# The second feed-forward matmul of seven token tiles as Strassen's seven block products

## The chip, the cores and the metric

One core of a Trainium2 chip. The metric is device microseconds of one execution; a kernel is run several times, beside runs of the kernel before on the same chip. Nearly all runs were fast. Fast runs of one kernel on one chip differ by up to about 1.5% (305.61 to 309.91 us for the kernel before).

In the views, PE is TensorE's matmuls, PEld its weight loads, DVE is VectorE, ACT ScalarE, POOL GpSimd and SP SyncE. A timeline line has start, length (both us), engine, source line, operation, output<-input, shapes and count; in brackets stands how long the engine was idle before it, and what ended that. "..." marks lines left out.

## The reference

Eight batches of eight heads do decayed linear attention ("retention") over 576 positions of width 64. The result, 4608 tokens of width 512, goes through a feed-forward block:

```python
ret = (q @ k.T / sqrt(64)) * gamma ** (i - j)   # i >= j, else 0
x = (ret @ v)                                    # 4608 x 512
h = x @ w_in                                     # 512 -> 2048
g = h * cos(h)
out = g @ w_out                                  # 2048 -> 512
```

## The kernel before

The tokens are handled in ten tiles n = 0 to 9, of 512 tokens (tiles 1 and 2: 256). Each tile has a first matmul, 8 blocks that fill a PSUM buffer of 128x1024 fp32 each (the text calls these buffers banks, by their names a, b, m, n and st), with a cosine on ScalarE and a multiply on VectorE behind every block, and a second matmul. The retention work of tile n + 1 is put between the matmuls of the second one: score matmuls, their mask products on VectorE, state matmuls, and "units" that do the output of two groups of 128 tokens.

```python
def mm1(n, et, c0, w, bank, inside={}):          # one block of the first matmul
    ...
    for j in range(m):
        for dg in range(DG):
            nc.tensor.matmul(ps[:, j, :], lhsT=w_in_sb[:, dg, ...], rhs=xT[:, dg, c0 : c0 + w], ...)
    cosh = cosp.tile([P, m, w], F32, tag="cosh", name="cosh")
    nc.scalar.activation(cosh, ps, ACTF.Sin, bias=half_pi, scale=1.0)
    nc.vector.tensor_mul(gT[:, et : et + m, c0 : c0 + w], ps, cosh)

def mm2(n, tsi, et, c0=0, c1=DM):                # one of 16 x 4 of the second matmul
    ...
    nc.tensor.matmul(ps, lhsT=gT[:, et, tsi * P : (tsi + 1) * P], rhs=w_out_sb[:, et, c0:c1], ...)
    if et == ET - 1:
        nc.scalar.copy(ot, ps)
        nc.sync.dma_start(out[...], ot)
        feed(s)                                  # more loads, preparations, transposes

def unit(g, bank, more=True, soon=False):
    attn_out([g, g + 1], bank, nc.scalar.copy)
    copy = states([g + 1, g + 2])()              # state matmuls into bank "st", additions on VectorE
    if more:
        scores2(g + 2)                           # scores into banks "a" and "b", then mask products
    copy()                                       # casts of the state, VectorE
# ... cut
```

GpSimd scales and casts q, k and v as they land (`prep`: two products of 1.04 us and a cast of 0.61 us for each group of 128 tokens). The program gives each engine its instructions in a fixed order, so an instruction that has to wait holds up those behind it in the same queue.

Of the kernel before, what the change touches and what calls it, by code (L numbers as in the profile page):

```python
# [8 lines left out]
F32 = mybir.dt.float32  # L9
# [4 lines left out]
ALU = mybir.AluOpType  # L14
# [3 lines left out]
def kernel(  # L18
# [38 lines left out]

    consts = ctx.enter_context(tc.tile_pool(name="consts", bufs=1))
    first = ctx.enter_context(tc.tile_pool(name="first", bufs=1))
    ld = ctx.enter_context(tc.tile_pool(name="ld", bufs=6))  # L60
    nat = ctx.enter_context(tc.tile_pool(name="nat", bufs=8))
    trp = ctx.enter_context(tc.tile_pool(name="trp", bufs=8))
    retp = ctx.enter_context(tc.tile_pool(name="retp", bufs=4))
    stp = ctx.enter_context(tc.tile_pool(name="stp", bufs=2))
    gp = ctx.enter_context(tc.tile_pool(name="gp", bufs=2))
    cosp = ctx.enter_context(tc.tile_pool(name="cosp", bufs=3))
    op = ctx.enter_context(tc.tile_pool(name="op", bufs=4))
    xp = ctx.enter_context(tc.tile_pool(name="xp", bufs=3))

    psum = ctx.enter_context(tc.tile_pool(name="psum", bufs=1, space=bass.MemoryType.PSUM))  # L70

# [150 lines left out]
        )  # L222
        tiles["sb", g + 1] = sb

    def states(gs):



        gs = [g for g in gs if g < NG and g % PER != PER - 1]
        if not gs:  # L230
            return lambda: (lambda: None)
        ps = psum.tile([P, len(gs), HG, D], F32, tag="st", name="st")
        for x, g in enumerate(gs):
            qks, vb, qkT, qT = tiles["a", g]
            vs = v_odd[:, g // PER % 2] if g % PER == MIX else vb
            for hg in range(HG):
                for he in range(2):
                    nc.tensor.matmul(  # L238
                        ps[he * D : he * D + D, x, hg, :],
                        lhsT=qks[:, 1, 2 * hg + he, :],  # L240
                        rhs=vs[:, 2 * hg + he, :],
                        start=(x == 0 and hg == 0),
                        stop=(x + 1 == len(gs) and hg == HG - 1),
                        skip_group_check=True,
                    )

        def copy():
            for g in gs:
                s, sb = tiles.pop(("s32", g)), blocks4[g % 4]
                for he in range(2):  # L250
                    r = slice(he * D, he * D + D)
                    nc.vector.tensor_copy(sb[r, :, r], s[r])  # L252
                tiles["sb", g + 1] = sb

        def add():
            for x, g in enumerate(gs):
                s = stp.tile([P, HG, D], F32, tag="s32", name="s32")
                if g % PER in (0, MIX):
                    nc.vector.tensor_copy(s, ps[:, x])  # L259
                else:  # L260
                    nc.vector.tensor_tensor(out=s, in0=ps[:, x], in1=tiles["s32"], op=ALU.add)  # L261
                tiles["s32"] = tiles["s32", g] = s
            return copy

        return add
# [61 lines left out]
        nc.scalar.activation(cosh, ps, ACTF.Sin, bias=half_pi, scale=1.0)  # L327
        nc.vector.tensor_mul(gT[:, et : et + m, c0 : c0 + w], ps, cosh)  # L328

    def mm2(n, tsi, et, c0=0, c1=DM):  # L330
        gT = tiles["g", n]
        if et == 0:
            bank = {0: "nmnm", 1: "nm", 2: "mn"}.get(n, "mnan")[tsi] if c0 == 0 else "ba"[c0 % DM // P % 2]
            tiles["o", tsi] = psum.tile([P, c1 - c0], F32, tag=bank, name="o")
        ps = tiles["o", tsi]
        nc.tensor.matmul(  # L336
            ps,
            lhsT=gT[:, et, tsi * P : (tsi + 1) * P],
            rhs=w_out_sb[:, et, c0:c1],
            start=(et == 0),  # L340
            stop=(et == ET - 1),
        )
        if et == ET - 1:
            ot = op.tile([P, c1 - c0], F32, tag="o", name="ot")
            nc.scalar.copy(ot, ps)  # L345
            s = starts[n] // P + tsi
            nc.sync.dma_start(out[s * P : (s + 1) * P, c0:c1], ot)
            feed(s)

    loaded = prepared = transposed = 4  # L350

# [144 lines left out]
    def unit(g, bank, more=True, soon=False):  # L496

        attn_out([g, g + 1], bank, nc.scalar.copy)
        copy = states([g + 1, g + 2])()
        if soon:  # L500
            copy()
        if more:
            scores2(g + 2)
        if not soon:
            copy()

    late = []
    for n, w in enumerate(widths):

        if n in (0, 3):  # L510
            halves = [(h, et) for et in range(0, ET, 4) for h in range(2)]
            if n == 3:
                halves.sort()
            blocks = [(et, half * 256, 256) for half, et in halves]
        elif n == 1:
            blocks = [(et, half * P, P) for half in range(2) for et in (0, 8)]
        else:
            blocks = [(et, 0, w) for et in range(0, ET, 1024 // w)]
        banks = {0: "abmabmab", 1: "bmba", 2: "bmab", 3: "mamabmab"}.get(n, "abmabmab")
        for i, (et, c0, cw) in enumerate(blocks):  # L520

            inside = {
                (0, 0): {2: lambda: (attn_out([3], "n"), state(3))},
                (1, 0): {4: lambda: scores(5, "a")},
                (1, 1): {3: lambda: attn_out([5], "a", evac=nc.scalar.copy)},
            }.get((n, i), {})
            mm1(n, et, c0, cw, banks[i], inside)
            if (n, i) == (3, 1):
                late.pop()()

        g = starts[n] // P + w // P
        if n == 0:
# [8 lines left out]
        elif n == 1:  # L541
            todo = pair(6, "ab", 16, 27)
        elif n == 2:
            todo = [(11, lambda: scores2(g)), (25, lambda: unit(g, "m", soon=True))]
            late += [lambda: unit(g + 2, "b", False)]
        elif n + 1 < len(widths):
            todo = [
                (20, lambda: unit(g, "m")),
                (52, lambda: unit(g + 2, "m", n > 3)),
            ]  # L550
            if n in (3, 4):
                todo[0] = (25, lambda: unit(g, "m"))
                todo.append((12, lambda: scores2(g)))
        else:
            todo = []
        todo.sort(key=lambda u: u[0])
        order, cols = [], [(0, DM)]
        for tsi in range(w // P):
            if (n + 1, tsi + 1) == (len(widths), w // P):
                cols = [(0, DM // 2), (DM // 2, 3 * DM // 4), (3 * DM // 4, DM)]  # L560
            order += [(tsi, et, c0, c1) for c0, c1 in cols for et in range(ET)]
        if n == 0:

            part = 3 * ET // 4
            order[: 2 * ET] = [
                (tsi, et, 0, DM)
                for tsi, et in [(t, e) for e in range(part) for t in range(2)]
                + [(t, e) for t in range(2) for e in range(part, ET)]
            ]
        for i, (tsi, et, c0, c1) in enumerate(order):  # L570
            while todo and todo[0][0] <= i:
                todo.pop(0)[1]()
            mm2(n, tsi, et, c0, c1)
        assert not todo


# [28 lines left out]
```

## Time and profile before

| | before |
|---|---|
| median of the first three runs | 309.84 us |
| median with the fourth, taken beside the changed kernel | 308.94 us |
| span of the profiled execution | 304.4 us |
| TensorE, VectorE, GpSimd busy | 97%, 57%, 33% |
| a late tile (6), first matmul to first matmul | 31.13 us |

From the page of the kernel before: busy time by engine, the granted TensorE clock in 40 slices (9 is full speed) and the chain of work that ended last, by engine.

```profile
span 304.4 us, 5826 instructions
...
PE 295.5 (97%) x2411; PEld 169.2 (56%) x2441; DVE 172.9 (57%) x215; ACT 128.2 (42%) x145; POOL 101.1 (33%) x127
...
PEclk9999999999999999999999999999999999999999
...
PE 92%; DMA 5%; issue 1%; SPq 1%; DVE 0%; POOL 0%; ACT 0%; ACTq 0%
```

TensorE is the bound: it is busy for 97% of the span; it is 92% of the chain.

One group of instructions, the multiplies of the first matmul (busy us, mean ns of one, idle before them):

```profile
L328 DVE TENSOR_TENSOR gT<-h,cosh 128x1024 bf16<-128x1024 f32 x72 | 88.2, 1225 | 54.4 <-ACT cosh L327 54.3
```

A group's mean for TensorE is a modelled duration (379 ns for 512 columns), not a pitch: for matmuls the spacing is read from the timeline, 215.9 ns for 512 columns and 109.2 ns for 256. The multiply of VectorE, 1.225 us, comes every 1.73 us in the first matmul, so 0.5 us of every block is free.

A line of the view of one source line, the casts of the state on VectorE, gives the shortest, the median and the longest duration; below it the timeline where GpSimd is busy, and then where it is not.

```profile
L252 DVE CAST sb<-s x48: 274/291/1182, 82.6 to 266.3; 64x256 bf16<-64x256 f32 x48
```

```profile
148.53 1.04 POOL L136 TENSOR_TENSOR qks<-fq,gq 128x512 bf16<-128x512 f32 x1 [2.23 <-DMA fq<-in_q_dram]
...
148.84 3.07 DVE L252 CAST sb<-s 64x256 bf16<-64x256 f32 x4
...
149.72 1.04 POOL L137 TENSOR_TENSOR qks<-fk,gk 128x512 bf16<-128x512 f32 x1
```

```profile
171.49 1.20 DVE L252 CAST sb<-s 64x256 bf16<-64x256 f32 x4
```

Four casts beside GpSimd's work took 3.07 us, four casts without it 1.20 us.

The table of stretches, one line for each of tiles 2, 3 and 4 (us, busy time and count of each engine, granted clock, DMA share, GB/s):

```profile
core 0: us, PE busy (x) PEld busy (x) DVE busy (x) ACT busy (x) POOL busy (x), PEclk, DMA share, GB/s
67.50:83.94 16.44, 16.22 (x163) 11.19 (x165) 9.28 (x13) 6.54 (x7) 8.08 (x9) 1.00 1.21 206
83.94:117.04 33.10, 32.73 (x342) 23.22 (x344) 23.90 (x32) 14.20 (x15) 16.73 (x19) 1.00 1.08 213
117.04:148.83 31.79, 31.26 (x242) 15.91 (x245) 18.56 (x20) 13.27 (x14) 14.34 (x17) 1.00 1.21 221
```

### The profile page before, as it was taken

The numbers are of one execution on the slowest core, as the hardware profiler recorded it, in microseconds if no ns is written. First come the engines' busy times: TensorE is split into PE (matmuls) and PEld (weight loads), VectorE is DVE, ScalarE is ACT, GpSimd is POOL, SyncE is SP. The second block draws the span as 40 slices with busy tenths as digits, with TensorE's granted clock in tenths as the row PEclk, the third lists the DMA queues.
The fourth block names the chain that finished last, engine by engine and source line by source line (L and its number), as shares of the span: only waits on it lengthen the run. The fifth ranks groups of instructions, "written<-read, shape, count | busy, mean of one in ns | idle before, by whom it ended". The sixth has DMA issues, their size and how long they took to land.

```text
span 304.4 us, 5826 instructions
## 1 busy us (share of the span) xinstructions
PE 295.5 (97%) x2411; PEld 169.2 (56%) x2441; DVE 172.9 (57%) x215; ACT 128.2 (42%) x145; POOL 101.1 (33%) x127
## 2 busy tenths in 40 slices
PE   8899999999999999999999999999999999999995
PEld 3578647758588554445544554455445544554444
DVE  5677514665687665774875566646765557504700
ACT  2656333515256224532364236422652255226511
POOL 2780076445346355444536253415330000000000
PEclk9999999999999999999999999999999999999999
DMA  8999999999989999999999999389923600020012
GB/s 208 202 209 207 208 219 194 220 228 203 209 181 207 220 216 248 228 221 195 223 242 223 187 263 196 49 196 210 254 35 86 89 34 2 34 71 34 0 71 69
DMA packets 150810, 50.19 MB, mean 165 GB/s; under 512 B 140800, under 2 KB 146304, under 8 KB 150784
## 3 DMA queue, kind: packets, MB, share of 16 engines
q1 hardware_dynamic: 146560, 45.63, 79.6%
q0 software_dynamic: 4224, 4.19, 8.4%
q8 instruction: 19, 0.31, 0.5%
q14 instruction: 7, 0.06, 0.1%
HBM read 36.70 MB, written 9.44 MB: 152 GB/s over the span
## 4 chain that ended last, share of the span: by engine, by line
PE 92%; DMA 5%; issue 1%; SPq 1%; DVE 0%; POOL 0%; ACT 0%; ACTq 0%
PE h L319 41%; PE o L336 40%; PE ov L292 3%; PE sc L179 3%; DMA w_in_sb<-in_moe_w_in_dram 2%; DMA fk<-in_k_dram 2%; PE ov L279 2%; PE st L238 1%; SPq L111 1%; PE st L208 0%; DVE xT L304 0%; POOL qks L137 0%; SPq L381 0%; PE tr L157 0%; ACT ot L345 0%
## 5 line engine op out<-in xcount | busy, mean ns | idle before, releaser
L336 PE MATMUL o<-w_out_sb,gT 128*128 128x512 bf16 (+2 forms) x586 | 126.2, 367 | 2.5 <-issue 2.2
L319 PE MATMUL h<-xT,w_in_sb 128*128 128x512 bf16 (+2 forms) x826 | 127.1, 313 | 0.7 <-DMA w_in_sb<-in_moe_w_in_dram 0.2
L328 DVE TENSOR_TENSOR gT<-h,cosh 128x1024 bf16<-128x1024 f32 x72 | 88.2, 1225 | 54.4 <-ACT cosh L327 54.3
L319 PEld LDWEIGHTS <-w_in_sb 128*128 128x128 bf16 x832 | 75.9, 98 | 50.4 <-issue 0.4
L327 ACT ACTIVATE cosh<-h,half_pi 128x1024 f32<-128x1024 f32 x72 | 80.2, 1113 | 51.3 <-PE h L319 51.3
L336 PEld LDWEIGHTS <-gT 128*128 128x128 bf16 x608 | 56.3, 98 | 62.0 <-issue 0.2
L136 POOL TENSOR_TENSOR qks<-fq,gq 128x512 bf16<-128x512 f32 x32 | 33.3, 1042 | 98.0 <-DMA fq<-in_q_dram 95.4
L345 ACT COPY ot<-o 128x512 f32<-128x512 f32 (+2 forms) x38 | 21.4, 563 | 86.4 <-PE o L336 86.3
L137 POOL TENSOR_TENSOR qks<-fk,gk 128x512 bf16<-128x512 f32 x35 | 36.5, 1043 | 16.2 <-DMA fk<-in_k_dram 14.4
L188 DVE TENSOR_TENSOR ret<-sc,tri 128x1024 bf16<-128x1024 f32 x32 | 38.0, 1218 | 4.1 <-PE sc L179 4.0
L304 ACT CAST xT<-ov 128x1024 bf16<-128x1024 f32 (+1 forms) x18 | 16.5, 917 | 21.4 <-PE ov L292 21.2
L143 POOL CAST vb<-fv 128x512 bf16<-128x512 f32 x32 | 19.6, 612 | 6.9 <-DMA fv<-in_v_dram 5.5
L261 DVE TENSOR_TENSOR s<-st,s 128x256 f32<-128x256 f32 x18 | 7.6, 424 | 24.3 <-PE st L238 24.0
L252 DVE CAST sb<-s 64x256 bf16<-64x256 f32 x48 | 19.2, 401 | 0.7
L292 PE MATMUL ov<-ret,vb 128*64 128x128 bf16 x288 | 12.0, 222 | 0.0
L217 DVE TENSOR_TENSOR sb<-st,diag 128x512 bf16<-128x512 f32 x8 | 5.5, 686 | 11.4 <-PE st L208 10.6
L259 DVE COPY s<-st 128x256 f32<-128x256 f32 x6 | 2.5, 424 | 15.8 <-PE st L238 15.8
L179 PEld LDWEIGHTS <-qkT 64*128 64x128 bf16 x288 | 8.1, 94 | 5.0 <-ACT qkT L162 2.3
L279 PEld LDWEIGHTS <-sb 128*128 128x128 bf16 x128 | 8.4, 98 | 3.8
L179 PE MATMUL sc<-qkT 64*128 64x128 bf16 x256 | 10.3, 217 | 0.0
L292 PEld LDWEIGHTS <-vb 128*64 128x64 bf16 x288 | 8.7, 109 | 2.0
L279 PE MATMUL ov<-qkT,sb 128*128 128x128 bf16 (+1 forms) x116 | 8.8, 215 | 0.1
(53 smaller groups left out, 76.3 us busy)
## 6 DMA issues: line engine op xcount, KB each, us to landing
out_dram<-ot SPq DMA_DIRECT2D x35, 256.0 KB, 4.2
fk<-in_k_dram SPq DMA_DIRECT2D x32, 256.0 KB, 4.8
fv<-in_v_dram SPq DMA_DIRECT2D x32, 256.0 KB, 5.0
fq<-in_q_dram SPq DMA_DIRECT2D x28, 256.0 KB, 4.1
w_in_sb<-in_moe_w_in_dram POOLq DMA_DIRECT2D x4, 512.0 KB, 8.6
w_out_sb<-in_moe_w_out_dram POOLq DMA_DIRECT2D x4, 512.0 KB, 15.9
fq<-in_q_dram SPq DMA_DIRECT2D x2, 512.0 KB, 4.4
fq<-in_q_dram SPq DMA_DIRECT2D x8, 128.0 KB, 4.2
```

The lines of the kernel that those rows point to most:

```text
L136: nc.gpsimd.tensor_tensor(out=qks[:, 0], in0=fq, in1=tq, op=ALU.mult)
L137: (nc.vector if g == 3 else nc.gpsimd).tensor_tensor(out=qks[:, 1], in0=fk, in1=tk, op=ALU.mult)
L143: nc.gpsimd.tensor_copy(vb, fv)
L179: nc.tensor.matmul(ps[:, he, hg, :], lhsT=qkT[d0 : d0 + D, HG + hg, :], rhs=qT[d0 : d0 + D, hg, :], start=True, stop=True,)
L188: nc.vector.tensor_tensor(out=ret.rearrange("p a b i -> p (a b) i"), in0=ps.rearrange("p a b i -> p (a b) i"), in1=mask.unsqueeze(1).to_br ...
L279: nc.tensor.matmul(ps[:, x, hg, :n], lhsT=sb[:, hg, :], rhs=qT[:, hg, :n], start=(hg == 0), stop=False, skip_group_check=True,)
L292: nc.tensor.matmul(ps[he * D : he * D + D, x, hg, :], lhsT=vb[:, 2 * hg + he, :], rhs=ret[:, he, hg, :], start=(g % PER == 0 and hg == 0), ...
L319: nc.tensor.matmul(ps[:, j, :], lhsT=w_in_sb[:, dg, (et + j) * P : (et + j + 1) * P], rhs=xT[:, dg, c0 : c0 + w], start=(dg == 0), stop=(d ...
L327: nc.scalar.activation(cosh, ps, ACTF.Sin, bias=half_pi, scale=1.0)
L328: nc.vector.tensor_mul(gT[:, et : et + m, c0 : c0 + w], ps, cosh)
L336: nc.tensor.matmul(ps, lhsT=gT[:, et, tsi * P : (tsi + 1) * P], rhs=w_out_sb[:, et, c0:c1], start=(et == 0), stop=(et == ET - 1),)
L345: nc.scalar.copy(ot, ps)
```

## The change

For the tiles from 3 on (`S7 = 3`), the second matmul `C = G W` is done in seven products of half-size blocks in place of eight. Blocks are sums of bf16 operands; products that share a sum stay in one fp32 PSUM chain. Products run in the order 3, 4, 5, 2, 1, 7, 6. Each needs a sum of two quarters of `gT` (five of seven do) or of `w_out` (made once; two of them in place).

```diff
+    def g_sum(n, x, e0, e1):
+        a, b, op_ = {
+            5: ((0, 0), (0, 1), ALU.add),       2: ((1, 0), (1, 1), ALU.add),
+            1: ((0, 0), (1, 1), ALU.add),       7: ((0, 1), (1, 1), ALU.subtract),
+            6: ((1, 0), (0, 0), ALU.subtract),
+        }[x]
+        ...
+        (nc.gpsimd if x in (6, 7) else nc.vector).tensor_tensor(
+            out=tiles["gs", n, x][:, e0:e1], in0=i0, in1=i1, op=op_
+        )
+    def sums_after(n, i):                       # behind block i of the first matmul
+        if n == S7:
+            if i < 4:
+                w_sums(3, 2 * i, 2 * i + 2)     # in place in w_out
+                w_sums(4, 2 * i, 2 * i + 2)
+            ready = {6: (0, 4), 7: (4, 8)}.get(i)
+        else:
+            ready = {1: (0, 2), 3: (2, 4), 5: (4, 6), 7: (6, 8)}.get(i)
+        if ready:
+            g_sum(n, 5, *ready)
+            g_sum(n, 2, *ready)
+            if ready[1] % 4 == 0:
+                g_sum(n, 7, ready[1] - 4, ready[1])
+                g_sum(n, 6, ready[1] - 4, ready[1])
+    def product(n, x):                          # 16 matmuls of 256 columns
+        ...
+    def mm2_seven(n, at):                       # products, PSUM reads, combinations, stores
+        for x in (3, 4, 5, 2, 1, 7, 6):
+            for u in at.get(x, []):
+                u()
+            product(n, x)
+            ...                                 # x == 5: also g_sum(n, 1, 0, E2) on VectorE
+    def unit7(g, more=True):
+        copy = states([g + 1, g + 2], "b")()    # states now in bank "b"
+        attn_out([g, g + 1], "m", nc.scalar.copy)
+        if more:
+            scores2(g + 2)
+        copy(nc.scalar.copy)                    # casts of the state now on ScalarE
@@ the loop over tiles
+            if n == 2 and i < 3:
+                for e in (0, 4):
+                    w_sums((1, 6, 7)[i], e, e + 4)
+                at = {5: [lambda: unit7(g)], 1: [lambda: unit7(g + 2, n > S7)]}
+                if n in (3, 4):
+                    at[4] = [lambda: scores2(g)]
+            mm2_seven(n, at)
```

(Excerpts: lines between are left out. Also cut: fewer buffers, `ld` 6 to 5, `gp` 2 to 1, `cosp` 3 to 2, `xp` 3 to 2, to make room for the sums; the shorter last store is gone.) The intent: TensorE bounds the kernel, so an eighth of the second matmul's columns less is time gained, and the sums go to engines with room.

More of the change, by code (lines that the diff above doesn't have):

```diff
@@ L59 @@
     first = ctx.enter_context(tc.tile_pool(name="first", bufs=1))
-    ld = ctx.enter_context(tc.tile_pool(name="ld", bufs=6))
+    ld = ctx.enter_context(tc.tile_pool(name="ld", bufs=5))
     nat = ctx.enter_context(tc.tile_pool(name="nat", bufs=8))
@@ L64 @@
     stp = ctx.enter_context(tc.tile_pool(name="stp", bufs=2))
-    gp = ctx.enter_context(tc.tile_pool(name="gp", bufs=2))
-    cosp = ctx.enter_context(tc.tile_pool(name="cosp", bufs=3))
-    op = ctx.enter_context(tc.tile_pool(name="op", bufs=4))
-    xp = ctx.enter_context(tc.tile_pool(name="xp", bufs=3))
+    gp = ctx.enter_context(tc.tile_pool(name="gp", bufs=1))
+    sump = ctx.enter_context(tc.tile_pool(name="sump", bufs=1))
+    cosp = ctx.enter_context(tc.tile_pool(name="cosp", bufs=2))
+    op = ctx.enter_context(tc.tile_pool(name="op", bufs=2))
+    xp = ctx.enter_context(tc.tile_pool(name="xp", bufs=2))
     psum = ctx.enter_context(tc.tile_pool(name="psum", bufs=1, space=bass.MemoryType.PSUM))
@@ L223, in state, with states @@
         tiles["sb", g + 1] = sb
-    def states(gs):
+    def states(gs, bank="st"):
         gs = [g for g in gs if g < NG and g % PER != PER - 1]
         if not gs:
-            return lambda: (lambda: None)
-        ps = psum.tile([P, len(gs), HG, D], F32, tag="st", name="st")
+            return lambda: (lambda *_: None)
+        ps = psum.tile([P, len(gs), HG, D], F32, tag=bank, name="st")
         for x, g in enumerate(gs):
@@ L245, in states, with copy @@
                     )
-        def copy():
+        def copy(run=nc.vector.tensor_copy):
             for g in gs:
@@ L251, in copy @@
                     r = slice(he * D, he * D + D)
-                    nc.vector.tensor_copy(sb[r, :, r], s[r])
+                    run(sb[r, :, r], s[r])
                 tiles["sb", g + 1] = sb
@@ L328, in mm1, with mm2 @@
         nc.vector.tensor_mul(gT[:, et : et + m, c0 : c0 + w], ps, cosh)
-    def mm2(n, tsi, et, c0=0, c1=DM):
+    def mm2(n, tsi, et):
         gT = tiles["g", n]
         if et == 0:
-            bank = {0: "nmnm", 1: "nm", 2: "mn"}.get(n, "mnan")[tsi] if c0 == 0 else "ba"[c0 % DM // P % 2]
-            tiles["o", tsi] = psum.tile([P, c1 - c0], F32, tag=bank, name="o")
+            bank = {0: "nmnm", 1: "nm", 2: "mn"}[n][tsi]
+            tiles["o", tsi] = psum.tile([P, DM], F32, tag=bank, name="o")
         ps = tiles["o", tsi]
@@ L338, in mm2 @@
             lhsT=gT[:, et, tsi * P : (tsi + 1) * P],
-            rhs=w_out_sb[:, et, c0:c1],
+            rhs=w_out_sb[:, et, :],
             start=(et == 0),
@@ L343, in mm2, with w_quarter @@
         if et == ET - 1:
-            ot = op.tile([P, c1 - c0], F32, tag="o", name="ot")
+            s = starts[n] // P + tsi
+            ot = op.tile([P, DM], F32, tag="oabcd"[1 + s % 4], name="ot")
             nc.scalar.copy(ot, ps)
-            s = starts[n] // P + tsi
-            nc.sync.dma_start(out[s * P : (s + 1) * P, c0:c1], ot)
+            nc.sync.dma_start(out[s * P : (s + 1) * P, :], ot)
             feed(s)
+    E2 = ET // 2
+    N2 = DM // 2
+    S7 = 3
+    w_sum = {}
+    def w_quarter(r, c):
+        return w_out_sb[:, r * E2 : (r + 1) * E2, c * N2 : (c + 1) * N2]
@@ new lines, in w_sums @@
+    def w_sums(x, e0, e1):
+        a, b, op_ = {
+            3: ((0, 1), (1, 1), ALU.subtract),
+            4: ((1, 0), (0, 0), ALU.subtract),
+            1: ((0, 0), (1, 1), ALU.add),
+            6: ((0, 0), (0, 1), ALU.add),
+            7: ((1, 0), (1, 1), ALU.add),
+        }[x]
+        if x in (3, 4):
+            w_sum[x] = w_quarter(*a)
+        elif x not in w_sum:
+            pool, tag = {1: (consts, "ws1"), 6: (first, "qs4"), 7: (first, "qT4")}[x]
+            w_sum[x] = pool.tile([P, E2, N2], BF16, tag=tag, name=f"ws{x}")
+        nc.vector.tensor_tensor(
+            out=w_sum[x][:, e0:e1],
+            in0=w_quarter(*a)[:, e0:e1],
+            in1=w_quarter(*b)[:, e0:e1],
+            op=op_,
+        )
@@ new lines, in g_sum @@
+    def g_sum(n, x, e0, e1):
+        gT = tiles["g", n]
+        a, b, op_ = {
+            5: ((0, 0), (0, 1), ALU.add),
+            2: ((1, 0), (1, 1), ALU.add),
+            1: ((0, 0), (1, 1), ALU.add),
+            7: ((0, 1), (1, 1), ALU.subtract),
+            6: ((1, 0), (0, 0), ALU.subtract),
+        }[x]
+        if ("gs", n, x) not in tiles:
+            tiles["gs", n, x] = sump.tile([P, E2, 256], BF16, tag=f"gs{x}", name=f"gs{x}")
+        i0, i1 = (
+            gT[:, k * E2 + e0 : k * E2 + e1, r * 256 : (r + 1) * 256] for r, k in (a, b)
+        )
+        (nc.gpsimd if x in (6, 7) else nc.vector).tensor_tensor(
+            out=tiles["gs", n, x][:, e0:e1], in0=i0, in1=i1, op=op_
+        )
@@ new lines, in product @@
+    def product(n, x):
+        gT = tiles["g", n]
+        if x in (3, 4, 1, 7):
+            ps = psum.tile([P, 2, N2], F32, tag={3: "n", 4: "st", 1: "n", 7: "st"}[x], name="o")
+            tiles["o", x] = ps
+        else:
+            ps = tiles["o", {5: 3, 2: 4, 6: 1}[x]]
+        lhs = {3: gT[:, :E2, :256], 4: gT[:, E2:, 256:]}.get(x)
+        if lhs is None:
+            lhs = tiles["gs", n, x]
+        rhs = {5: w_quarter(1, 1), 2: w_quarter(0, 0)}.get(x)
+        if rhs is None:
+            rhs = w_sum[x]
+        for e in range(E2):
+            for j in range(2):
+                nc.tensor.matmul(
+                    ps[:, j],
+                    lhsT=lhs[:, e, j * P : (j + 1) * P],
+                    rhs=rhs[:, e, :],
+                    start=(x in (3, 4, 1, 7) and e == j == 0),
+                    stop=(e == E2 - 1 and j == 1),
+                    skip_group_check=True,
+                )
@@ new lines, in mm2_seven, with new, store @@
+    def mm2_seven(n, at):
+        s0 = starts[n] // P
+        def new(tag):
+            return op.tile([P, 2, N2], F32, tag=tag, name="ot")
+        def store(t, r, c, s):
+            r0 = starts[n] + r * 256
+            nc.sync.dma_start(
+                out[r0 : r0 + 256, c * N2 : (c + 1) * N2].rearrange("(j p) c -> p j c", p=P), t
+            )
+            feed(s)
+        for x in (3, 4, 5, 2, 1, 7, 6):
+            for u in at.get(x, []):
+                u()
+            product(n, x)
+            if x == 3:
+                u22 = new("a")
+                nc.scalar.copy(u22, tiles["o", 3])
+            elif x == 4:
+                u11 = new("b")
+                nc.scalar.copy(u11, tiles["o", 4])
+                nc.gpsimd.tensor_tensor(out=u22, in0=u22, in1=u11, op=ALU.add)
+            elif x == 5:
+                c12 = new("c")
+                nc.scalar.copy(c12, tiles["o", 3])
+                nc.gpsimd.tensor_tensor(out=u11, in0=u22, in1=c12, op=ALU.subtract)
+                g_sum(n, 1, 0, E2)
+                store(c12, 0, 1, s0)
+            elif x == 2:
+                c21 = new("d")
+                nc.scalar.copy(c21, tiles["o", 4])
+                nc.gpsimd.tensor_tensor(out=u22, in0=u22, in1=c21, op=ALU.subtract)
+                store(c21, 1, 0, s0 + 1)
+            elif x == 1:
+                nc.vector.tensor_tensor(out=u11, in0=tiles["o", 1], in1=u11, op=ALU.add)
+            elif x == 7:
+                nc.vector.tensor_tensor(out=u11, in0=tiles["o", 7], in1=u11, op=ALU.add)
+                store(u11, 0, 0, s0 + 2)
+            elif x == 6:
+                nc.vector.tensor_tensor(out=u22, in0=tiles["o", 1], in1=u22, op=ALU.add)
+                store(u22, 1, 1, s0 + 3)
@@ L517 @@
         else:
-            blocks = [(et, 0, w) for et in range(0, ET, 1024 // w)]
+            m = 1024 // w
+            blocks = [(et, 0, w) for et in range(0, ET, m)]
+            if n > S7:
+                blocks = [(e + k * E2, 0, w) for e in range(0, E2, m) for k in range(2)]
         banks = {0: "abmabmab", 1: "bmba", 2: "bmab", 3: "mamabmab"}.get(n, "abmabmab")
@@ L529 @@
                 late.pop()()
+            if n == 2 and i < 3:
+                for e in (0, 4):
+                    w_sums((1, 6, 7)[i], e, e + 4)
+            if n >= S7:
+                sums_after(n, i)
         g = starts[n] // P + w // P
@@ L545 @@
             late += [lambda: unit(g + 2, "b", False)]
-        elif n + 1 < len(widths):
-            todo = [
-                (20, lambda: unit(g, "m")),
-                (52, lambda: unit(g + 2, "m", n > 3)),
-            ]
-            if n in (3, 4):
-                todo[0] = (25, lambda: unit(g, "m"))
-                todo.append((12, lambda: scores2(g)))
-        else:
-            todo = []
-        todo.sort(key=lambda u: u[0])
-        order, cols = [], [(0, DM)]
-        for tsi in range(w // P):
-            if (n + 1, tsi + 1) == (len(widths), w // P):
-                cols = [(0, DM // 2), (DM // 2, 3 * DM // 4), (3 * DM // 4, DM)]
-            order += [(tsi, et, c0, c1) for c0, c1 in cols for et in range(ET)]
+        else:
+            at = {}
+            if n + 1 < len(widths):
+                at = {5: [lambda: unit7(g)], 1: [lambda: unit7(g + 2, n > S7)]}
+                if n in (3, 4):
+                    at[4] = [lambda: scores2(g)]
+            mm2_seven(n, at)
+            continue
+        todo.sort(key=lambda u: u[0])
+        order = [(tsi, et) for tsi in range(w // P) for et in range(ET)]
         if n == 0:
             part = 3 * ET // 4
-            order[: 2 * ET] = [
-                (tsi, et, 0, DM)
-                for tsi, et in [(t, e) for e in range(part) for t in range(2)]
-                + [(t, e) for t in range(2) for e in range(part, ET)]
+            order[: 2 * ET] = [(t, e) for e in range(part) for t in range(2)] + [
+                (t, e) for t in range(2) for e in range(part, ET)
             ]
-        for i, (tsi, et, c0, c1) in enumerate(order):
+        for i, (tsi, et) in enumerate(order):
             while todo and todo[0][0] <= i:
                 todo.pop(0)[1]()
-            mm2(n, tsi, et, c0, c1)
+            mm2(n, tsi, et)
         assert not todo
```

## The prediction

> **What bounds the kernel now.** TensorE: 295.5 of 304.4 us busy (97%, busy-time table); the chain of waits that ended last is 92% TensorE. In the timeline a late tile takes about 31.2 us: 13.8 us first matmul (64 of 512 columns, 215.9 ns apart), 13.8 us second, about 3.7 us retention work. VectorE is 57% busy, GpSimd 33%.
>
> **What the change removes.** 64 matmuls of 512 columns per tile become 112 of 256. The 256-column ones of the first matmul ran 109.2 ns apart (96 in 10.65 us), so 12.2 us instead of 13.8: 1.6 us a tile, 11 us over seven, all on the critical path. Weight loads (98 ns) still fit beneath.
>
> **What it adds (estimates from trace durations).**
> - VectorE: eight 512-element bf16 sums per tile inside the first matmul, about 0.4 us each at double rate (the Trainium skill, "VectorE: DVE Perf Modes", perf-mode tier table; no bf16 sum is in this trace), one of 2048 (1.2 us), three combinations from PSUM (0.69 each). The multiplies gT<-h,cosh last 1.225 us and come every 1.73 us, so 0.5 us is free per block; the sums take 0.4 of it. A block's PSUM bank is free only 0.9 us before TensorE wants it.
> - GpSimd: four sums of 1024 (about 2.1 us each, from 1.04 us for 512) and three of 512: about 11 us a tile on top of 11.
> - State casts move to ScalarE, which has room.
>
> **The term that decides.** The Trainium skill ("SBUF — State Buffer", "SBUF: two separate sides") says a VectorE instruction with two SBUF inputs and a GpSimd instruction that reads SBUF exclude each other for a whole instruction. The trace shows that exclusion for VectorE's casts L252: 0.29 us median, 1.18 us longest; four take 1.20 us with GpSimd idle, 3.07 us with it busy. All new VectorE sums have two SBUF inputs. Twice a tile GpSimd becomes ready for a 2.1 us sum just as VectorE starts a pair of its own; the second of the pair should wait. I estimate 1 to 1.5 us of TensorE stall late in the first matmul (waiting for gT<-h,cosh to free a bank) and about 1.2 us before the score matmuls (bank b waits for the state additions): 2 to 3 us a tile, more than saved.
>
> **Once-only costs.** Tile 2: six weight sums (0.69 each) between four multiplies delay the score matmuls about 2.7 us. Tile 3: in-place weight sums, and states sharing bank b with scores just issued: about 4 to 7 us. Tile 4: 2 to 4 us, same bank. Tail: the last store is no longer cut into quarters; about 1.8 us.
>
> **Sum.** Without exclusion: -11 + 10 = about 308.5 us. With the full exclusion: about 325 to 330. I expect part: 316 us, 8 in 10 between 302 and 331. Faster by over 2%: 0.20; within 2%: 0.32; slower: 0.48.
>
> **What would show it.** Second-product matmuls 109 ns apart. VectorE sums in two groups of duration, 0.4 us and well above 1 us, the long ones overlapping GpSimd. TensorE busy below 93%, with waits of L320 and the scores on VectorE. Tile period 31 to 33 us, 29.8 if there is no exclusion.
>
> **What would make it wrong.** If two-input sums don't exclude GpSimd, or GpSimd's bf16 sums take half my estimate: below 305 us. If VectorE's sums run at single rate (0.69 us), or GpSimd falls so far behind that loads and transposes arrive late: above 331.

## The result

The changed kernel took 330.17 us (median of 4 runs, 328.02 to 331.04), the kernel before 308.94 us. The ratio is 1.0684 (95% interval 1.0631 to 1.0738). A ratio in this text is the mean time of one kernel's fast runs over that of the other's in the same rounds, so it is not quite the ratio of the medians quoted. The output is correct.

From the page of the changed kernel:

```profile
span 328.5 us, 6623 instructions
...
PE 296.4 (90%) x2724; PEld 202.0 (61%) x2745; DVE 238.1 (73%) x269; ACT 143.4 (44%) x183; POOL 195.9 (60%) x176
...
PEclk9999999998999789997999999999999999999999
```

TensorE's busy time is 296.4 us, not smaller than before, although it has fewer columns to do; the clock line has slices at 7. VectorE has 65 us more, GpSimd 95 us. The groups:

```profile
L329 DVE TENSOR_TENSOR gT<-h,cosh 128x1024 bf16<-128x1024 f32 x72 | 86.9, 1218 | 29.8 <-ACT cosh L328 29.5
...
L395 POOL TENSOR_TENSOR gs<-gT 128x1024 bf16<-128x1024 bf16 x28 | 63.4, 2284 | 45.3 <-DVE gT L329 45.3
...
L395 DVE TENSOR_TENSOR gs<-gT 128x512 bf16<-128x512 bf16 x48 | 44.1, 960 | 0.8
```

The small VectorE sums have a mean of 0.96 us; the shortest is 0.41. A sum of 1024 on GpSimd takes 2.28 us. The multiplies are as fast as before, only later. The longest waits by pair of engines (us in total, times, longest):

```profile
PE h L320 <- DVE gT L329: 6.9, 7, 1.4
...
PE st L239 <- DVE ret L189: 4.7, 2, 2.8
...
PE sc L180 <- DVE gT L329: 3.3, 3, 1.9
```

Every matmul stall of over 1 us waits for VectorE: the first and the second matmul for a multiply, the state matmuls for mask products, the scores for a multiply, and one product of the last tile for a sum. The timeline of tile 5 shows why VectorE is late:

```profile
176.61 2.69 DVE L395 TENSOR_TENSOR gs<-gT 128x512 bf16<-128x512 bf16 x2
176.66 4.62 POOL L395 TENSOR_TENSOR gs<-gT 128x1024 bf16<-128x1024 bf16 x2 [1.87 <-DVE gT L329]
...
179.22 2.34 DVE L329 TENSOR_TENSOR gT<-h,cosh 128x1024 bf16<-128x1024 f32 x2
...
180.49 1.89 PE L320 MATMUL h<-xT,w_in_sb 128*128 128x512 bf16 x8 [1.37 <-DVE gT L329]
```

VectorE's two small sums start at 176.61 and take 2.69 us in place of 0.76; GpSimd's first sum starts 0.05 us later, released by the same multiply, and lies between them. The next two multiplies end 2 us late, and TensorE stands 1.37 us for the bank that they free. (GpSimd's line shows two sums merged, 4.62 us.)

By tile, from the start of one first matmul to the next (the last one to TensorE's end), in us, read from the timelines:

| tile | before | after | difference |
|---|---|---|---|
| 2 | 16.44 | 21.61 | +5.2 |
| 3 | 33.10 | 39.52 | +6.4 |
| 4 | 31.79 | 37.73 | +5.9 |
| 5 | 31.36 | 33.85 | +2.5 |
| 6 | 31.13 | 31.88 | +0.8 |
| 7 | 31.37 | 32.45 | +1.1 |
| 8 | 30.67 | 31.54 | +0.9 |
| 9 | 27.87 | 28.93 | +1.1 |
| from TensorE's end to the end of the span | 3.2 | 4.1 | +0.9 |

The sum is about 24.7 us; the changed kernel started its first tile 0.6 us earlier, so the spans differ by 24.1 us. The medians differ by 21.2 us only: the profiled execution of the kernel before was a quick one. (Times are about 1.9 us longer than spans, so 304.4 us stands for some 306.3, less than any of its four timed runs.) The differences of the table may so be about 3 us too large in sum. None of tiles 2 to 9 got shorter. The stretches of tiles 2, 3 and 4 in the changed kernel, as those of before:

```profile
66.89:88.50 21.61, 17.91 (x162) 11.58 (x164) 14.65 (x18) 6.54 (x7) 11.15 (x11) 0.92 1.20 198
88.50:128.02 39.52, 34.63 (x394) 29.27 (x393) 32.28 (x40) 17.90 (x24) 29.24 (x24) 0.91 1.05 193
128.02:165.75 37.73, 32.65 (x292) 21.61 (x292) 28.54 (x29) 15.59 (x20) 26.49 (x24) 0.95 0.85 156
```

In tiles 2 to 4 the granted clock is 0.92, 0.91 and 0.95. What precedes a lower clock shows in three stretches of tile 3, after a wait of 1.92 us (107.57 to 109.49) and around one of 1.85 us (112.54 to 114.39):

```profile
109.00:112.00 3.00, 2.51 (x23) 1.95 (x23) 3.00 (x4) 0.00 (x0) 2.90 (x3) 0.80 1.28 264
112.00:114.40 2.40, 0.55 (x5) 0.09 (x4) 2.24 (x2) 0.58 (x1) 2.40 (x2) 0.50 1.17 214
114.40:117.70 3.30, 3.30 (x57) 2.78 (x58) 1.19 (x3) 0.88 (x1) 3.30 (x3) 0.51 1.10 202
```

In stretches of 1 us the clock is 1.00 up to 110, 0.89 in the next, then 0.50, 0.69 from 117 to 118 and 1.00 after: half from about 110.8 to 117.6 us, through the second stall and through 3.3 us in which TensorE worked all the time. The other two half-clock stretches, in tiles 2 and 4, also begin within 2 us of the end of a stall, and the profiled execution before has neither such stalls nor a half clock inside the tiles. A stall so costs more than itself: by the three means, tiles 2 to 4 lost some 7 us of full clock, an estimate and an upper limit, since part of it was idle anyway. In tile 4 the longest matmul stall of the kernel came about like this:

```profile
146.58 4.62 POOL L395 TENSOR_TENSOR gs<-gT 128x1024 bf16<-128x1024 bf16 x2 [2.63 <-DVE gT L329]
146.88 2.34 DVE L395 TENSOR_TENSOR gs<-gT 128x512 bf16<-128x512 bf16 x1
...
149.14 2.34 DVE L189 TENSOR_TENSOR ret<-sc,tri 128x1024 bf16<-128x1024 f32 x2
...
151.63 0.37 PE L239 MATMUL st<-vb,qks 128*64 128x64 bf16 x8 [2.83 <-DVE ret L189]
```

GpSimd's sums hold VectorE's next sum for 2.34 us; only then come the mask products, which must read bank b before the state matmuls may write it: 2.83 us of standing.

### The profile page after: what moved, and what is told of

It is laid out like the page before. It is cut to its first block, busy times and chain, and to the rows that moved or that the text cites. A ratio compares the mean times of both kernels' runs of the same rounds, so it can differ in the third digit from the quotient of the medians.

```text
span 328.5 us, 6623 instructions
## 1 busy us (share of the span) xinstructions
PE 296.4 (90%) x2724; PEld 202.0 (61%) x2745; DVE 238.1 (73%) x269; ACT 143.4 (44%) x183; POOL 195.9 (60%) x176
## 5 line engine op out<-in xcount | busy, mean ns | idle before, releaser
L395 POOL TENSOR_TENSOR gs<-gT 128x1024 bf16<-128x1024 bf16 x28 | 63.4, 2284 | 45.3 <-DVE gT L329 45.3
L395 DVE TENSOR_TENSOR gs<-gT 128x512 bf16<-128x512 bf16 (+2 forms) x59 | 61.3, 1076 | 0.8
L431 PEld LDWEIGHTS <-gs 128*128 128x128 bf16 x560 | 53.8, 98 | 9.0 <-DVE gs L395 1.5
L431 PE MATMUL o<-ws,gs 128*128 128x256 bf16 x336 | 37.9, 273 | 1.2 <-DVE gs L395 1.2
L337 PE MATMUL o<-w_out_sb,gT 128*128 128x512 bf16 x121 | 30.1, 391 | 2.7 <-DVE gT L329 2.3
L431 PE MATMUL o<-w_out_sb,gT 128*128 128x256 bf16 x224 | 27.2, 278 | 3.2 <-DVE gT L329 3.2
L431 PEld LDWEIGHTS <-gT 128*128 128x128 bf16 x224 | 21.6, 99 | 8.4 <-DVE gT L329 3.7
L431 PE MATMUL o<-w_out_sb,gs 128*128 128x256 bf16 x224 | 25.8, 274 | 0.0
L305 ACT CAST xT<-ov 128x1024 bf16<-128x1024 f32 (+1 forms) x18 | 16.5, 917 | 20.1 <-PE ov L293 20.0
L337 PEld LDWEIGHTS <-gT 128*128 128x128 bf16 x128 | 12.0, 100 | 16.2 <-DVE gT L329 2.4
L253 ACT CAST sb<-s 64x256 bf16<-64x256 f32 x40 | 16.1, 403 | 0.6
L468 POOL TENSOR_TENSOR ot<-ot 128x512 f32<-128x512 f32 x7 | 10.2, 1464 | 8.0 <-ACT ot L467 7.8
```

The costliest lines, as they stand in the source:

```text
L305: evac(tiles["x", n][:, :, t0 : t0 + len(gs) * P].rearrange("p c (x i) -> p x c i", i=P), ps)
L395: (nc.gpsimd if x in (6, 7) else nc.vector).tensor_tensor(out=tiles["gs", n, x][:, e0:e1], in0=i0, in1=i1, op=op_)
L431: nc.tensor.matmul(ps[:, j], lhsT=lhs[:, e, j * P : (j + 1) * P], rhs=rhs[:, e, :], start=(x in (3, 4, 1, 7) and e == j == 0), stop=(e == ...
```

## The experiments

Ten kernels were run. Theory: VectorE's sums (two SBUF inputs) and GpSimd's instructions that read SBUF exclude each other, and VectorE, with 0.1 us of slack for each block, hands the delay to TensorE. Rivals: VectorE has simply too much to do, or has it in the wrong order; or tiles 2 to 4 are slow for reasons of their own.

### The disputed cost by itself: m_port

A bench with nothing of the reference in it (wrong result): eight VectorE sums `V = G[:, :512] + G[:, 1024:1536]`, four GpSimd sums of 1024, fills of 1024, multiplies with one operand in PSUM and casts, alone and side by side, each phase started by ScalarE writing a few elements of the inputs.

> A bench, not the reference's computation (wrong result on purpose). VectorE bf16 sums of two 512-element SBUF operands alone, GpSimd sums of 1024 alone, then both at once, then VectorE sums beside GpSimd fills (which only write), VectorE multiplies with one PSUM and one SBUF operand beside GpSimd sums, and VectorE casts of 512 fp32 alone, beside sums and beside fills. Exclusion theory: sums alone about 0.4 us; beside GpSimd sums the eight VectorE sums take turns with them, so that some of them last over 2 us and the two engines together need the sum of their times (about 8 x 0.4 + 4 x 2.1 = 11.6 us for the part where both have work); beside fills about 0.4 us; the PSUM multiplies stay at 1.2 us. Rival (VectorE is only slow because it has much to do and waits for its inputs): all VectorE sums last 0.4 us in every phase.

The timeline, in order: VectorE's sums alone; GpSimd's sums alone; both; VectorE's sums beside fills; VectorE's PSUM multiplies beside fills, then beside sums; last, VectorE's casts of 512 fp32 elements beside fills.

```profile
15.30 2.71 DVE L60 TENSOR_TENSOR V<-G 128x512 bf16<-128x512 bf16 x8
...
18.53 8.33 POOL L69 TENSOR_TENSOR R<-G 128x1024 bf16<-128x1024 bf16 x4 [10.88 <-ACT G L56]
...
27.23 10.45 DVE L60 TENSOR_TENSOR V<-G 128x512 bf16<-128x512 bf16 x8 [9.22 <-ACT G L56]
27.34 9.05 POOL L69 TENSOR_TENSOR R<-G 128x1024 bf16<-128x1024 bf16 x4 [0.47 <-ACT G L56]
...
38.11 2.77 DVE L60 TENSOR_TENSOR V<-G 128x512 bf16<-128x512 bf16 x8 [0.44 <-ACT G L56]
38.20 7.21 POOL L72 MEMSET R<- 128x1024 bf16 x8 [1.81 <-ACT G L56]
...
41.53 9.14 DVE L63 TENSOR_TENSOR V<-ps,F 128x1024 bf16<-128x1024 f32 x8 [0.65 <-ACT F L57]
45.37 8.36 POOL L69 TENSOR_TENSOR R<-G 128x1024 bf16<-128x1024 bf16 x4
...
65.09 6.94 DVE L66 CAST V<-F 128x512 bf16<-128x512 f32 x8 [0.32 <-ACT F L57]
...
66.02 9.23 POOL L72 MEMSET R<- 128x1024 bf16 x8 [1.87 <-ACT G L56]
```

Eight sums alone take 2.71 us, four GpSimd sums alone 8.33 us, together VectorE needs 10.45 us: nearly the 11.04 us of their sum. Beside fills VectorE needs 2.77 us. Multiplies with a PSUM operand take 9.14 us for eight, 1.14 each, beside fills and sums alike. So the exclusion is real; for VectorE's sums, with both inputs in SBUF, it takes a GpSimd instruction that reads; and the engines take turns, one instruction each: four of the eight sums last 2.33 us, each to just behind the end of a GpSimd sum, the others 0.41 to 0.43. The rival that VectorE's sums are long for want of inputs is out. The phases with casts ran into each other (my start signal read only one slot of the output), but the trace has every instruction, and single ones tell something. A cast has one SBUF input. With GpSimd idle it lasts 0.41 us, beside GpSimd's sums 2.33, and beside fills, which read nothing, 1.25, while the fills go from 0.95 to 1.22. So casts exclude fills too, which the sums do not: the line of casts in the trace of the kernel before was a near relative of the case at hand, not the case itself.

### GpSimd's sums made to read nothing: e1_write_only

```diff
+        if x in (6, 7):
+            for _ in range(2):
+                i = nc.gpsimd.memset(tiles["gs", n, x][:, e0:e1], 0.5)
+                # waits for the same multiply as the sum did
+            return
-        (nc.gpsimd if x in (6, 7) else nc.vector).tensor_tensor(
+        nc.vector.tensor_tensor(
```

> GpSimd's four sums of gT per tile are replaced by two fills each (0.95 us each, so about 1.9 us busy in place of 2.2), released by the same multiply; they write the same tiles but read nothing. Wrong result on purpose (products 6 and 7 get constants). Exclusion theory: VectorE's 512-element sums fall from 0.96 us mean to 0.5 or less, only the preparations of q, k, v still collide; tiles 5 to 8 take 29.8 to 30.6 us in place of 31.5 to 33.9, tiles 3 and 4 lose some us too; in all 313 to 321 us. Rival (VectorE's added work and its order, not the exclusion): GpSimd is as busy as before, so 327 us or more.

313.09 us against 309.40 us for the kernel before on that chip: ratio 1.0111 (1.0047 to 1.0174). Wrong result. The groups of GpSimd's fills and VectorE's small sums:

```profile
L397 POOL MEMSET gs<- 128x1024 bf16 x56 | 52.4, 952 | 39.0 <-DVE gT L329 37.4
...
L406 DVE TENSOR_TENSOR gs<-gT 128x512 bf16<-128x512 bf16 x48 | 20.1, 459 | 0.8
```

The small sums fall from 960 to 459 ns on the mean. Tiles 4 to 9 lose 5.3, 3.6, 1.8, 2.2, 2.2 and 2.7 us, tiles 2 and 3 only 0.6 and 1.0. So of the 1.068 the exclusion by GpSimd's four sums is by far the most (330.17 less 313.09, about 17 us, from two sets of runs), and tiles 5 to 8 now beat the kernel before, in its quick profiled execution, by 1.0 to 1.4 us each, which is what the seven products are worth. Two small doubts: fills were busy 1.9 us for a sum's 2.3, and products 6 and 7 had constant weights. What is left over, 3.7 us and the gain that should have been there, lies almost all in tiles 2 and 3. In tile 2 of the changed kernel the same exclusion is at work with GpSimd's preparations, which this run leaves in place: its six weight sums last 0.67 to 1.53 us, 6.4 us in all in place of about 4.

### All sums on VectorE: e2_all_vector

```diff
-            if ready[1] % 4 == 0:
-                g_sum(n, 7, ready[1] - 4, ready[1])
-                g_sum(n, 6, ready[1] - 4, ready[1])
-        (nc.gpsimd if x in (6, 7) else nc.vector).tensor_tensor(
+        nc.vector.tensor_tensor(
                 g_sum(n, 1, 0, E2)
+                g_sum(n, 7, 0, E2)              # after product 5
+                g_sum(n, 6, 0, E2)              # after product 2
```

> All five sums of gT on VectorE; sums 7 and 6 as one instruction of 2048 each, after sum 1 and after product 2. VectorE gets about 2.4 us more work per tile, GpSimd 8.8 us less. Exclusion theory: the removed 2.2 us exclusions are worth more than the added work, tiles 5 to 8 take about 30 to 30.8 us, in all 315 to 322 us. Rival (VectorE's volume of work is what delays TensorE): tiles get longer by up to 2.4 us, 332 to 345 us.

334.31 us, ratio 1.0821 (1.0753 to 1.0888): my expectation missed, and the number is the one that the rival gave. The first matmul no longer stalls in tiles 5 to 8 (13.98 us in one piece), but:

```profile
187.11 5.41 DVE L395 TENSOR_TENSOR gs<-gT 128x2048 bf16<-128x2048 bf16 x3
...
192.44 0.94 DVE L262 TENSOR_TENSOR s<-st,s 128x256 f32<-128x256 f32 x2
...
193.52 0.61 PE L180 MATMUL sc<-qkT 64*128 64x128 bf16 x8 [3.19 <-DVE s L262]
```

Three sums of 2048 stand in VectorE's queue before the state additions of the second unit. The score matmuls wait 3.19 us for those additions, since they share bank b, and the clock of the stretch from 190 to 196 us is 0.75. The volume of the sums was not measured here. Nor is this run free of exclusion: 14 of the 21 sums of 2048 last 2.06 to 2.32 us, not 1.22, beside GpSimd's preparations and combinations, as the 5.41 us for three above show. So it moved the sums onto other GpSimd work and to a worse place in the queue, and doesn't separate the two.

### The seven products from tile 5 on: e3_from_five

`S7 = 5`; tiles 3 and 4 use the old second matmul and units, the two weight sums in place move to tile 5, the six others stay in tile 2.

```diff
-    S7 = 3
+    S7 = 5
+        elif n < S7:
+            todo = [(12, lambda: scores2(g)), (25, lambda: unit(g, "m")), (52, lambda: unit(g + 2, "m", n > 3))]
```

> Seven products from tile 5 on only; tiles 3 and 4 are again as in the kernel before (weight sums of tile 2 stay, the two in place move to tile 5). If the once-only costs belong to tiles 3 and 4 (scores late in the second matmul, bank b shared by scores and states, half clock after the stalls): tile 3 back to 33.1 and tile 4 to 31.8 us, tile 5 about 34 to 35, in all 316 to 320 us. If they belong to starting the seven products at all, they move into tile 5: 325 us or more.

318.08 us, ratio 1.0282 (1.0232 to 1.0333), as the first theory expected: tile 3 takes 33.11 and tile 4 31.79 us, as before, and tile 5 33.48. The once-only costs of tiles 3 and 4, where scores are made inside the second matmul, do not move on. Both tiles take their old time with the smaller buffers, so these aren't what slowed them. What of tile 3 is due to the weight sums in place and what to bank b was not taken apart.

### The weight sums moved out of tile 2: e4_wsums_later

```diff
-            if n == 2 and i < 3:
-                for e in (0, 4):
-                    w_sums((1, 6, 7)[i], e, e + 4)
+            if n == 3:                          # at steps 36, 42, 47 of the second matmul
+                todo += [(i, lambda x=x: (w_sums(x, 0, 4), w_sums(x, 4, 8))) for x, i in ((1, 36), (6, 42), (7, 47))]
```

> As the run that starts the seven products at tile 5, but the six weight sums of tile 2 move into the second matmul of tile 3, where VectorE has room. If those six sums in front of the multiplies are what made tile 2 take 21.6 us: tile 2 back to 16.5 us, tile 3 at most 1 us longer, total 318.1 - 5 = 312.5 to 314 us. If tile 2 was slow for another reason (fewer buffers of gT, cosh or loads): 317 to 318 us.

321.19 us, ratio 1.0450 (1.0365 to 1.0534): worse than without the move, a miss. Tile 2 went from 20.51 to 19.10 us only: now its scores wait 2.67 us for a transpose of qk by DMA, which the slower tile had hidden. And tile 5, which has the same instructions in both kernels, went from 33.48 to 38.57 us:

```profile
162.46 2.67 DVE L373 TENSOR_TENSOR w_out_sb<-w_out_sb 128x512 bf16<-128x512 bf16 x2
...
162.62 4.49 POOL L395 TENSOR_TENSOR gs<-gT 128x1024 bf16<-128x1024 bf16 x2 [1.83 <-DVE gT L329]
...
165.06 2.66 DVE L395 TENSOR_TENSOR gs<-gT 128x512 bf16<-128x512 bf16 x2
...
168.91 3.34 PE L320 MATMUL h<-xT,w_in_sb 128*128 128x512 bf16 x8 [4.43 <-DVE gT L329]
```

Here GpSimd's preparations came at other moments, so that GpSimd's two sums met first the pair of weight sums and then the pair of gT sums: 2.67 and 2.66 us for two pairs of 0.75, and a stall of 4.43 us. This tile was caught by the same exclusion with another phase; how much it costs depends on what GpSimd happens to do.

### All sums on VectorE, but placed: e5_late_five

From tile 5 on, weight sums as in the run before; sum 5 behind the last multiply, sum 2 behind the state additions of the first unit, sum 1 behind its mask products, sums 7 and 6 behind the second unit's state additions.

```diff
+    def unit7(g, more=True, sums=lambda: None):
         attn_out([g, g + 1], "m", nc.scalar.copy)
+        sums()
         if more:
             scores2(g + 2)
+            first7 = lambda: unit7(g, True, lambda: late_sums(2))
+            second7 = lambda: unit7(g + 2, True, lambda: late_sums(7, 6))
+            at = {5: [first7, lambda: late_sums(1)], 1: [second7]}
```

> As the run before, and all five sums of gT on VectorE, whole and behind the first matmul: sum 5 before the first unit, sum 2 between the state additions and the mask products of that unit, sum 1 after them, sums 7 and 6 behind the second unit's state additions (not in front of them, where they cost 3.2 us a tile in the all-VectorE run); the last tile keeps small early pieces. Exclusion and order theory: no stall in the first matmul (13.8 us), tiles 5 to 8 take 29.8 to 30.4 us, 304 to 307 us in all. Rival (VectorE's volume decides): tiles 5 to 8 as in the all-VectorE run, 33 us and more, over 316 us.

312.34 us, ratio 1.0165 (1.0078 to 1.0252; by the 2% rule the verdict is unclear): better than with GpSimd's sums, but 5 us above what I expected. The first matmul is 13.98 us in each of tiles 5 to 9, and a new wait has come:

```profile
213.49 2.34 DVE L189 TENSOR_TENSOR ret<-sc,tri 128x1024 bf16<-128x1024 f32 x2
...
215.75 0.68 DVE L474 TENSOR_TENSOR ot<-o,ot 128x512 f32<-128x512 f32 x1
...
216.48 1.91 PE L429 MATMUL o<-ws,gs 128*128 128x256 bf16 x16 [2.32 <-DVE ot L474]
```

Product 6 adds to bank n, which VectorE must first read for product 1; that reading stood behind two mask products.

### The units of tiles 3 and 4 one product later: e6_unit_later

```diff
-                    at[4] = [lambda: scores2(g)]
+                    at = {4: [lambda: scores2(g)], 2: at[5], 7: at[1]}
```

> The changed kernel, but in tiles 3 and 4 the two retention units run one product later each (before product 2 and product 7), so that the state matmuls, which write bank b, come 1.75 us later after the scores that VectorE must first read out of it. If the shared bank is the cause of the 1.85 and 2.83 us stalls there and of the half clock behind them: tiles 3 and 4 together 3 to 6 us shorter, 324 to 327 us. If VectorE is simply that far behind (sums and exclusion in front of the mask products): the stall only moves, 329 to 331 us.

328.86 us, ratio 1.0684 (1.0604 to 1.0763), one slow run left out. Tile 4 is 3.1 us shorter, but tile 3 is 0.7 and tile 6 is 1.3 us longer. The stall before the states went from 1.85 to 0.84 us in tile 3, and a new one of 1.90 us came before its scores. The ratio is that of the changed kernel: the second reading, that VectorE is behind and the stall moves, holds better than the first.

### Placed sums from tile 4 on: e7_late_four

`S7 = 4` in the kernel with placed sums, with tile 4's units one product later.

> As the run with late sums, from tile 4 on, with tile 4's units one product later. One more tile of about 1.3 us saved, less what tile 4's scores inside the second matmul and the two weight sums in place cost there: 303 to 308 us. If tile 4 stalls as in the changed kernel: 309 us or more.

320.22 us, ratio 1.0411 (1.0342 to 1.0480), 8 us worse than from tile 5. Tile 4 takes 36.25 us; product 1 waits 2.30 us and product 7 1.46 us for sums. (The first tile of this profile was 1.5 us longer, which belongs to the start. Tile 2 then took 16.25 us and its scores waited for no transpose: the wait of 2.67 us above, and one of 2.05 in the run before last, seem to depend on when the loads come, not on the seven products.) It seems that a tile with an extra pair of mask products inside its second matmul has no room on VectorE for five sums; this was not taken apart.

### The placed sums with the last two mends: e8_best

```diff
-            second7 = lambda: unit7(g + 2, True, lambda: late_sums(7, 6))
-            at = {5: [first7, lambda: late_sums(1)], 1: [second7]}
+            second7 = lambda: unit7(g + 2, False, lambda: late_sums(7, 6))
+            at = {5: [first7, lambda: late_sums(1)], 1: [second7], 7: [lambda: scores2(g + 4)]}
-    ... sump.tile(..., tag=f"gs{x}")
+    ... sump.tile(..., tag=f"gs{ {7: 5, 6: 2}.get(x, x) }")
-    ld = ... bufs=5
+    ld = ... bufs=6
```

> The run with late sums from tile 5, with two mends. The mask products of the second unit are issued behind the combination of product 1 in VectorE's queue (there product 6 waited 1.9 to 2.3 us for that combination, which frees bank n); and sums 7 and 6 reuse the memory of sums 5 and 2, so that loads have six buffers again as before (the score matmul of tile 2 waited 2.05 us for a transpose). If VectorE's order is what was left: no wait of product 6 over 0.5 us, tiles 5 to 7 take 30.2 to 31.4 us in place of 32.6 to 33.3, 304 to 308 us in all, within 2 per cent of the kernel before. If the five sums are simply too much beside the retention work, the wait moves to the next matmul: 310 us or more.

307.04 us against 308.26 us, five rounds: ratio 0.9941 (0.9891 to 0.9991). The wait of product 6 is 0.25 us:

```profile
180.04 1.91 PE L429 MATMUL o<-ws,gs 128*128 128x256 bf16 x16 [0.25 <-DVE ot L474]
```

Tiles 5 to 8 take 31.86, 30.30, 31.05 and 30.44 us. The result is correct; this version is 7% faster than the changed kernel and, by about a half of a per cent, than the kernel before, with an interval that only just leaves out no difference. The two mends were made together. The sixth load buffer did little: the scores of tile 2 still wait 1.75 us for a transpose.

### From tile 5 on, without GpSimd's reads: e9_five_write

The kernel of the third experiment with the fills of the first (wrong result).

> Seven products from tile 5 on as in that run, with GpSimd's sums of gT as fills that read nothing (wrong result on purpose). Exclusion by GpSimd's sums explains tiles 5 to 9: they take 30.1 to 30.4 us (29.3 for tile 8) as in the other write-only run, so 318 - 6 to - 9 = 309 to 312 us, what is left over the kernel before being tile 2 with its weight sums and the tail. If the exclusion mattered only together with tiles 3 and 4: 316 us or more.

307.89 us, ratio 0.9990 (0.9947 to 1.0033), somewhat better than expected. Tiles 5 to 9 take 32.67, 30.08, 30.27, 29.31 and 26.20 us. Between this and the third experiment lie only GpSimd's reads (and 0.4 us less busy time for each sum): 318.08 to 307.89 us, on different chips; the ratio falls from 1.0282 to 0.9990.

## Why the prediction was wrong

- **The bound and the gain: right in kind, a little large.** Seven products of 256-column matmuls do shorten a tile, and the weight loads do fit. But the matmuls ran 111 ns apart on the mean when the seams between products are counted (16 x 7 in 12.45 us, tile 6 of the write-only run), so a tile is worth about 1.3 us, not 1.6; whole tiles were 1.0 to 1.4 us shorter in that run.
- **The mechanism: right.** "All new VectorE sums have two SBUF inputs" and "the second of the pair should wait" describe the lines at 176.61 us as they are. Of the 48 small sums 31 lasted 0.41 to 0.54 us, 13 lasted over 2 us, and 4 lay between; TensorE was 90% busy; tiles 6 to 8 took 31.5 to 32.5 us, within the 31 to 33 forecast. One link was loose: the casts that it leans on have one SBUF input, so they did not show the two-input case; the bench did.
- **The step that failed: "I expect part: 316 us".** The text had summed the full exclusion to "about 325 to 330" and then took less than half of the difference to the sum without it, on no evidence of the trace. That left 7.5 us for the exclusion (316 less 308.5), with the full version at 16.5 to 21.5; the write-only run puts it at about 17 us. The bench shows why: where both engines have such work, they need the sum of their times. The measured 330.17 us is the upper end of the full sum and only just inside the stated range, but far from the point that was forecast. That the full sum comes so close is in part luck: it took the exclusion at up to 21.5 us, and all the rest 4.6 us too low (308.5 for 313.09).
- **"Without exclusion: -11 + 10 = about 308.5 us"** was too low: without GpSimd's reads the kernel took 313.09 us (309.40 for the kernel before). The mis-sized terms are the gain, 7 times 1.3, about 9 us and not 11, and of the once-only costs that of tile 2: 2.7 us forecast, 4.5 in the write-only run. Gross of the 1.3 us that a tile of seven products gains, tile 3 cost 6.8 us there (5.5 + 1.3; 4 to 7 forecast) and tile 4 2.0 (0.7 + 1.3; 2 to 4 forecast), as foreseen; but the sum had taken 10 us for costs that, with 1.8 for the tail, come to 10.5 to 15.5. With GpSimd's sums the same terms were 5.2, 7.7 (6.4 + 1.3) and 7.2 us (5.9 + 1.3), so of tile 4's cost 5.3 us is exclusion.
- **What those terms left out.** Three things. After stalls of 2 to 3 us TensorE's clock was half for some us; no such stall was in the trace before, and the sum had no term for it. The exclusion also struck the mask products' place in the queue, ahead of bank b: the write-only run takes 5.3 us off tile 4 alone. And the weight sums of tile 2 met GpSimd's preparations: 6.4 us in place of about 4.
- **The tail** was forecast at 1.8 us and cost 0.9.
- **"Single rate" and "loads arrive late"**, the two ways to be above 331 us, did not happen: the shortest 512-element sum is 0.41 us, and only one long wait for a transpose showed, when tile 2 was made faster.
- **What stays open:** how tile 3's 6.4 us divide between weight sums in place, bank b and the clock; and how much more than a half per cent a better place for the weight sums and the DMA of tile 2 would give.

## What to carry to other kernels

Work moved to "idle" engines is not free if two of them exclude each other: VectorE's bf16 sums of two SBUF operands and GpSimd's instructions that read SBUF ran one after the other here (10.45 us for 2.71 and 8.33), and VectorE's casts did so even with fills (1.25 us for 0.41), so add their times before you call either idle. When an in-order engine feeds the bound engine with less than 1 us of slack, look at the place of a new instruction in its queue before its length, and put it behind whatever frees a PSUM bank: with the same five sums all on VectorE, tiles 5 to 7 took 35 to 36 us, then 32.6 to 33.3, then 30.3 to 31.9 as the sums and mask products were moved (the first of these with seven products from tile 3 on). And if an estimate has a full and a half version, look for the line in the trace that chooses between them before splitting the difference; here the casts at 148.84 us, the longest of which lasted 1.18 us beside a GpSimd product of 1.04, were the nearest thing to that line.

## What the Trainium skill lacked or had wrong

- "SBUF — State Buffer", section "Who interferes with whom": right in all that the runs tried (8 sums 2.71 us alone, 10.45 us beside GpSimd sums, 2.77 us beside fills; PSUM multiplies unchanged; casts 0.41 us alone, 1.25 us beside fills). It says that the later one blocks, but not who goes on when both have several in a row: the runs show turns of one instruction each, so a pair of 0.76 us takes 2.69 us with one GpSimd sum between.
- "GPSIMD Engine Reference", section "Performance versus the Vector engine": it gives 4497 ns for a sum of 2048 in fp32 and no figure for bf16. Here 1024 in bf16 took 2.08 us (8.33 us for four), against 2.25 us as an estimate from half of that figure, so the narrower type hardly helps.
- "VectorE: DVE Perf Modes", section on the perf-mode tier table: the double rate of a bf16 sum holds, 0.41 us for 512 and 1.22 us for 2048 elements when undisturbed; that such a sum waits up to 1.9 us longer beside GpSimd isn't said in that table, only on the page above.
- "TensorE: Matmul & The Clock Gate", section "What's actually happening", puts the half clock after at least one idle window of about 3.4 us; a later section allows for frequent short gaps, without a length. Here it came after shorter gaps with work between them: in tile 3 1.92 us idle up to 109.49 us, then 1.3 us of matmuls, and half clock from about 110.8 us on; and in tile 4 from about 151.7 us, behind a gap of 2.83 us that ended at 151.63 and some us after one of 1.91 us.
